# One change to a loop of 64 recurrent attention segments: order of scores and V, the last K in two banks, batched Q/K groups in 32-column tiles, and other issue times for three transfers

## The chip, the cores and the metric

The kernel runs on one core of a Trainium2 chip. The metric is device time of one execution in microseconds; before the change it is 854.24 us, the median of 3 runs (854.01 to 854.5).

The core has TensorE (matmul; its result goes to the eight banks of PSUM, each 512 fp32 values for each of 128 partitions), VectorE, ScalarE and GpSimd, which work on tiles in SBUF, and DMA queues. All transfers of this kernel are issued in program order by SyncE (SP). In the profile PE is TensorE's matmuls, PEld its weight loads, DVE is VectorE, ACT ScalarE, POOL GpSimd.

## What is computed

Two residual blocks in a row, A (attention with a small memory that is carried from segment to segment) and B (a gated MLP that mixes over the sequence). S = 2048 rows of 512, 32 heads of 128, 8 memory rows, segments of 32 rows: 64 segments that must run one after the other. Cut to what matters:

```python
def A(x, mem0, Wq, Wk, Wv, Wo):              # x: layernormed input
    mem = mem0
    for s in range(64):
        h = concat([mem, x[32 * s:32 * s + 32]])       # 8 + 32 rows
        q, k, v = h @ Wq, h @ Wk, h @ Wv               # 32 heads of 128
        p = softmax(mask(q @ k.T * 128 ** -0.5))       # memory columns open, the rest causal
        o = (p @ v) @ Wo
        mem = o[:8]
        out.append(o[8:])

def B(x, w_in, w_sp, b_sp, w_out):           # x: layernormed
    z = gelu(x @ w_in)                       # 512 -> 1792
    z2 = layernorm(z[:, 896:])
    return (z[:, :896] * (w_sp @ z2 + b_sp[:, None])) @ w_out

h = x + A(layernorm(x), ...)
out = h + B(layernorm(h), ...)
```

## The kernel before

All engines' programs are written out by hand, fully unrolled. A small emitter derives the semaphore waits: each operation names the tokens that it reads and writes (`reads=`, `writes=`, `after=`), and waits for their last writer or readers. Two engines that read one PSUM bank are also put in order. So each engine runs its operations in the order in which the Python code emits them.

**Layout.** A segment has 40 rows, 8 of memory and 32 of x. The loop works on 32 of them as one tile: the 8 memory rows and the first 24 rows of x (`hT`, transposed, 4 chunks `dc` of 128 of the 512 inputs). The last 8 rows of x of each segment ("extra rows") don't need the memory, so their Q, K and V are computed ahead for 16 segments at once, 128 rows: a "chunk" `ck`, 4 in all. Q and K of extra rows end in `QTx` (two buffers), V in DRAM (`vext_d`), from where `load_vx` brings one segment's rows into one of 3 slots of `Vx`.

**32-column tiles.** With 32 rows a weight tile has 32 columns, so four matmuls with `tile_position` (0, 32c) share the array, each with its own 512 columns: a "quad". `tile_mm` with `held` leaves out the weight load where the same `hT` chunk is loaded already.

**One turn of the loop** (L945 to L1112), in TensorE's order:

- `QK(s, b, mi, ...)`: Q (mi 0) and K (mi 1) of the heads' halves b = 0, 1, each four quads into its bank of `QKB`; between them the second half of `mem_out` brings the memory rows of the segment before. `QK_evac` copies a bank into `Tst` on ScalarE, with pairs of heads side by side as 4-byte words, and VectorE transposes 32x32 blocks of these words into `QT` and `KT`. The last K half (b = 1) is copied and transposed in two parts.
- `S_half(s, b)`: scores of a half, onto a mask that VectorE has put into the bank; `sm_exp` (ScalarE), `sm_sums` (matmuls with ones), `sm_ln` and `sm_rcp` (ScalarE; the reciprocal is exp(-ln)), `sm_norm` (GpSimd for half 0, VectorE for half 1; each a wide and a narrow multiplication).
- `V_half`: V of half b, four quads into banks 6 and 2; `V_evac` copies them on VectorE.
- one group of side work, from a list `gx`: in s = 1 to 7, 14 and 15 V of extra rows (`vx_group`), in the other turns below 48 Q or K of extra rows (`qkx_group`: 16 matmuls with 128-column weights of one head each and 128 moving rows), from 48 on a half row block of B's z2 (`z2_group`). Single quads of such work (`gv`) are poured in at one or two other places of a turn.
- `PV_half` for both halves, `cT_evac`, then `WoX_mm` (the output projection of extra rows, two quads), `Wo` into banks `OB` and `OB2`, `part_evac`, `mem_out`, and one more piece of side work by s mod 4.

**Transfers in the loop**, in SP's order: every second turn `wT_piece` transposes 64 rows of `B_w_sp` by DMA into `wst` and stores them to `wT_d` (32 pieces); rows of x and h; at the end of a turn V rows for s + 2; from s = 32 on B's weights and transposed rows. After the loop come `load_wT(0)` (the first quarter of the mixing weights, 8 transfers into what was w_q) and the z2 rows that had been stored.

Of the kernel before, what the change touches and what calls it, by code (L numbers as in the profile page):

```python
# [169 lines left out]
def fast_path(nc, st, keep, A_x, A_mem0, A_Wq, A_Wk, A_Wv, A_Wo, A_seg_len, B_w_in, B_w_sp, B_b_sp, B_w_out, out):  # L170
# [15 lines left out]
    CK = 16  # L186
# [24 lines left out]
    QTx = [region(4 * WSZ + i * QX, QX).rearrange("p (m s h k) -> p m s h k", m=2, s=CK, h=H) for i in range(2)]  # L211
# [206 lines left out]
    def qkx_evac(ck, i, bank, eng="act"):  # L418
        mi, h0 = i // 8, 4 * (i % 8)
        dst = QTx[ck % 2][:, mi, :, h0:h0 + 4, :].rearrange("p s h k -> p h s k")  # L420
# [60 lines left out]
    QKB = {(0, 0): 0, (0, 1): 1, (1, 0): 6, (1, 1): 7}  # L481
    SBK = (0, 1)
# [29 lines left out]
    def QK_evac(s, b, mi, parts=1):  # L512
        bank = QKB[(b, mi)]
        tb = mi
        n = 8 // parts
        for k in range(parts):
            tok = [("T", tb, 0), ("T", tb, 1)] if parts == 1 else [("T", tb, k)]
            cs = slice(64 * n * k, 64 * n * (k + 1))
            act(lambda e, cs=cs: e.activation(out=Tst[:, tb, cs].rearrange("p (hp i r) -> p hp i r", i=32, r=2),  # L519
                                              in_=ps[:, bank, cs].rearrange("p (hp r i) -> p hp i r", r=2, i=32), func=ACT.Copy),  # L520
                reads=[PB(bank)], writes=tok)
        for k in range(parts):
            tok = [("T", tb, 0), ("T", tb, 1)] if parts == 1 else [("T", tb, k)]
            src = Tst[:, tb, 64 * n * k:64 * n * (k + 1)].bitcast(U32)
            hs = slice(n * k, n * (k + 1))
            if mi == 0:
                dst = QT[:, b, hs, :, :].rearrange("p hp q r -> p (hp q r)").bitcast(U32).rearrange("p (hp q) -> p hp q", hp=n)[:, :, 8:40]
                wr = [("QT", b)]
            else:
                dst = KT[:, b, hs, :, :].rearrange("p hp q r -> p (hp q r)").bitcast(U32)  # L530
                wr = [("KT", b, 0), ("KT", b, 1)] if parts == 1 else [("KT", b, k)]
            dve(lambda e, dst=dst, src=src: e.transpose(out=dst, in_=src), reads=tok, writes=wr)  # L532
# [66 lines left out]

    def V_half(s, b, dcs=range(DC), held=None):  # L600
        bank = VB[b]
        sl = slot(s)
        for dc in dcs:
            for c in range(4):
                c0 = (16 * b + 4 * c) * DH
# [305 lines left out]
    for ck, i0 in ((1, 10), (2, 0), (3, 0)):  # L911
# [3 lines left out]
        for i in range(i0, 16):  # L915
            qkx_group(ck, i)
# [1191 lines left out]
```

## Time and profile before

| what | value |
|---|---|
| median of 3 runs | 854.24 us |
| the profiled execution, its own time | 853.86 us |
| its span in the profile | 851.7 us |
| busy: TensorE matmul | 837.0 us, 98% of the span |
| busy: VectorE | 538.8 us, 63% |
| busy: ScalarE | 427.1 us, 50% |
| busy: GpSimd | 159.8 us, 19% |
| mean DMA rate | 91 GB/s |
| loop: first scores of s = 1 to first scores of s = 63 | 57.67 to 686.76 us |
| granted TensorE clock | full in all slices |

The page's share of TensorE counts each matmul from its start to a modelled end, and matmuls of different tiles overlap. In the timeline a row is a run of like instructions with start, length and count; the distance from the start of one row to the start of the next is what the row cost.

### The profile page before, as it was taken

To read this page: it belongs to the slowest core of one execution; us is meant where nothing else is said; L and a number is where in the kernel's file an instruction comes from. 1 tells how busy PE (TensorE), PEld (TensorE's weight loads), DVE (VectorE), ACT (ScalarE), POOL (GpSimd) and SP (SyncE) were. 2 spreads that over 40 slices of the span, in tenths; PEclk is the share of its full clock that TensorE was granted. 3 is DMA by queue.
4 is the path that set the end of the run, shared out by engine and by line. 5 is a ranking of instruction groups with operands and counts; after the bars stand their busy time and mean duration, and the time that the engine had idled before them with its cause. 6 is when DMAs were issued, how large, how long until landed. Compare 5 with 4: busy or idle time off the path is not lost.

```text
span 851.7 us, 43893 instructions
## 1 busy us (share of the span) xinstructions
PE 837.0 (98%) x20921; PEld 447.0 (52%) x19133; DVE 538.8 (63%) x1256; ACT 427.1 (50%) x1151; POOL 159.8 (19%) x404
## 2 busy tenths in 40 slices
PE   6999999999999999999999999999999999999997
PEld 5754445555555555556555555555554544444443
DVE  3456677676666666676766666767666676553443
ACT  2455565656555655555655555565656566500000
POOL 5111121122121112121212121211112123200000
PEclk9999999999999999999999999999999999999999
DMA  9972322223212122121323222233322369032001
GB/s 319 379 227 59 75 56 57 54 47 82 57 34 75 34 65 62 26 72 47 64 58 85 55 74 51 81 70 85 91 57 80 96 184 366 2 112 105 33 12 40
DMA packets 105614, 77.21 MB, mean 91 GB/s; under 512 B 63304, under 2 KB 90960, under 8 KB 105424
## 3 DMA queue, kind: packets, MB, share of 16 engines
q1 hardware_dynamic: 105424, 74.35, 30.3%
q8 instruction: 159, 2.61, 1.3%
q14 instruction: 31, 0.25, 0.1%
HBM read 42.38 MB, written 21.59 MB: 75 GB/s over the span
## 4 chain that ended last, share of the span: by engine, by line
PE 95%; DMA 2%; SPq 1%; issue 0%; ACT 0%; DVE 0%; POOL 0%; POOLq 0%
PE f_ps L495 46%; PE f_ps L1183 11%; PE f_ps L496 8%; PE f_ps L414 6%; PE f_ps L707 4%; PE f_ps L1300 3%; PE f_ps L623 3%; PE f_ps L1176 2%; PE f_ps L433 2%; PE f_ps L775 2%; PE f_ps L554 1%; PE f_ps L575 1%; DMA f_arena<-in_A_Wk_dram 1%; PE f_ps L629 1%; PE f_ps L439 1%; PE f_ps L680 1%
## 5 line engine op out<-in xcount | busy, mean ns | idle before, releaser
L495 PE MATMUL f_ps<-f_arena,f_hT 128*32 128x512 bf16 x5120 | 359.5, 380 | 0.3
L495 PEld LDWEIGHTS f_ps<-f_arena,f_hT 128*32 128x32 bf16 x5120 | 117.0, 95 | 153.7 <-issue 63.0
L519 ACT ACTIVATE f_Tst<-f_ps 128x512 bf16<-128x512 f32 (+1 forms) x320 | 150.0, 510 | 77.5 <-PE f_ps L495 77.4
L495 PE MATMUL f_ps<-f_arena,f_cT 128*32 128x256 bf16 x3844 | 127.9, 272 | 0.7 <-ACT f_cT L642 0.5
L495 PEld LDWEIGHTS f_ps<-f_arena,f_cT 128*32 128x32 bf16 x3844 | 94.8, 96 | 27.3 <-ACT f_cT L642 18.2
L615 DVE CAST f_V_sb<-f_ps 128x512 bf16<-128x512 f32 x128 | 88.6, 692 | 25.4 <-PE f_ps L495 25.4
L1183 PE MATMUL f_ps<-f_arena 128*128 128x512 bf16 x448 | 100.9, 379 | 0.6 <-DMA f_arena<-wT_d 0.6
L532 DVE STREAM_TRANSPOSE f_QT<-f_Tst 128x256 uint32<-128x256 uint32 x128 | 57.0, 446 | 68.6 <-ACT f_Tst L519 68.5
L496 PE MATMUL f_ps<-f_arena,f_hT 128*32 128x512 bf16 x1024 | 99.8, 379 | 0.0
L539 POOL COPY f_QT<-f_arena 128x256 bf16<-128x256 bf16 x64 | 30.8, 482 | 313.3 <-PE f_ps L560 313.2
L642 ACT ACTIVATE f_cT<-f_ps 128x320 bf16<-128x320 f32 x128 | 49.0, 435 | 49.1 <-PE f_ps L629 49.1
L644 DVE TENSOR_SCALAR f_cT<-f_ps 128x320 bf16<-128x320 f32 x128 | 56.9, 487 | 25.4 <-PE f_ps L629 25.4
L532 DVE STREAM_TRANSPOSE f_KT<-f_Tst 128x128 uint32<-128x128 uint32 (+1 forms) x192 | 64.5, 349 | 12.9 <-ACT f_Tst L519 12.9
L1183 PEld LDWEIGHTS f_ps<-f_arena 128*128 128x128 bf16 x448 | 43.7, 98 | 53.4 <-DVE f_mv L723 1.0
L673 DVE CAST f_part<-f_ps 128x256 bf16<-128x256 f32 x64 | 27.2, 425 | 67.9 <-PE f_ps L495 67.9
L414 PE MATMUL f_ps<-f_hTe,f_arena 128*128 128x128 bf16 x1024 | 66.9, 223 | 2.2 <-DMA f_arena<-in_A_Wq_dram 1.4
L414 PEld LDWEIGHTS f_ps<-f_hTe,f_arena 128*128 128x128 bf16 x1024 | 59.1, 100 | 7.5 <-ACT f_hTe L395 1.6
L586 ACT ACTIVATE f_R_sb<-f_ps 128x160 f32<-128x160 f32 x128 | 39.1, 305 | 35.9 <-PE f_ps L496 32.7
L1189 DVE TENSOR_TENSOR f_arena<-f_ps,f_arena 128x512 f32<-128x512 f32 x28 | 19.3, 690 | 52.9 <-PE f_ps L1183 52.9
L685 ACT ACTIVATE f_hT<-f_ps 128x16 bf16<-128x16 f32 x126 | 23.3, 185 | 53.4 <-PE f_ps L680 53.0
L671 ACT ACTIVATE f_part<-f_ps 128x256 bf16<-128x256 f32 x64 | 24.6, 385 | 48.4 <-PE f_ps L495 48.4
L544 DVE CAST f_ps<-f_mask 128x224 f32<-128x224 bf16 x128 | 47.1, 368 | 0.0
(118 smaller groups left out, 1094.1 us busy)
## 6 DMA issues: line engine op xcount, KB each, us to landing
wT_d<-f_wst SPq DMA_DIRECT2D x32, 256.0 KB, 2.5
f_arena<-wT_d SPq DMA_DIRECT2D x32, 256.0 KB, 4.8
f_arena<-in_A_Wq_dram SPq DMA_DIRECT2D x4, 1024.0 KB, 8.7
f_arena<-in_A_Wk_dram SPq DMA_DIRECT2D x4, 1024.0 KB, 14.3
f_arena<-in_A_Wv_dram SPq DMA_DIRECT2D x4, 1024.0 KB, 14.5
f_arena<-in_A_Wo_dram SPq DMA_DIRECT2D x8, 512.0 KB, 9.5
f_Vx<-vext_d SPq DMA_DIRECT2D x63, 64.0 KB, 2.9
vext_d<-f_Vs SPq DMA_DIRECT2D x24, 128.0 KB, 2.0
```

The source lines that it names most:

```text
L414: pe(lambda e, h=h, dc=dc, hh=hh: e.matmul(ps[:, bank, hh * 128:(hh + 1) * 128], lhsT=ws[:, dc, h * DH:(h + 1) * DH], rhs=hTe[:, ck % 3, d ...
L495: return e.matmul(out, lhsT=lhsT, rhs=rhs, start=start, stop=stop, skip_group_check=True, tile_position=(0, 32 * c))
L496: return e.add_instruction(mybir.InstMatmult(name=nc.get_next_instruction_name(), ins=[e.lower_ap(rhs), e.lower_ap(lhsT)], outs=[e.lower_a ...
L519: act(lambda e, cs=cs: e.activation(out=Tst[:, tb, cs].rearrange("p (hp i r) -> p hp i r", i=32, r=2), in_=ps[:, bank, cs].rearrange("p (h ...
L532: dve(lambda e, dst=dst, src=src: e.transpose(out=dst, in_=src), reads=tok, writes=wr)
L544: dve(lambda e: e.tensor_copy(out=ps[:, bank, 0:224], in_=mask[:, :]), reads=["mask"], writes=[PB(bank)])
L586: act(lambda e: e.activation(out=R_sb[:, b, :], in_=ps[:, bank, 224:384], func=ACT.Ln, scale=LNS), reads=[PB(bank)], writes=[("R", b)])
L615: dve(lambda e: e.tensor_copy(out=V_sb[:, b, :], in_=ps[:, bank, :]), reads=[PB(bank)], writes=[("V", b)])
L642: act(lambda e: e.activation(out=dst, in_=src, func=ACT.Copy, scale=UNSC), reads=[PB(PVB[c])], writes=[("cT", c)])
L644: dve(lambda e: e.tensor_scalar(out=dst, in0=src, scalar1=UNSC, scalar2=None, op0=ALU.mult), reads=[PB(PVB[c])], writes=[("cT", c)])
L707: pe(lambda e, h=h, g=g, i=8 * qr + bg: e.matmul(ps[32 * g:32 * g + 32, WXB, :], lhsT=cTx[:, rb % 2, i, :], rhs=w_o[:, h, :], start=(i < 4 ...
L1183: pe(lambda e: e.matmul(ps[:, bank, 0:TB], lhsT=z2[:, sc, fb * 128:(fb + 1) * 128], rhs=wTb[tb % 2][:, :, sc, :], start=(n == 0), stop=(n ...
```

## The change

Seven edits, with the loop's mathematics unchanged:

1. **Order of the first QK quads.** Q and K of half 0 take chunk 0, then chunk 1, together, so that weights are held.
2. **K of half 1 in two banks** (`K1`, `K1_copy`, `K1_transpose`): 8 half-quads of 256 columns into banks 3 and 7 in place of four quads into bank 7.
3. **Order of scores, V and softmax.** Before the first sums stand four V quads (two chunks of half 0 less one, and one of half 1) in place of five, the last V quad of half 0 follows the second scores, the last one of half 1 the second sums. The second exp precedes the first ln.
4. **V copies and norms.** The copy of half 1 is split between VectorE and ScalarE; the narrow norm of half 0 goes from GpSimd to VectorE.
5. **Batched Q/K groups** (`qkr_group`): 36 of the 38 groups of extra rows in the loop take 32 rows of 4 segments and 16 heads as four quads of 512 columns, evacuated like QK by `pair_copy` on ScalarE and a transposition on VectorE. For this the heads are paired in another order, `QTx` has pairs side by side, and `qx_copy` moves 4-byte words.
6. **w_sp in halves.** 64 half pieces of 1024 columns, one a turn (two in s = 6 and 10), each issued after the first part of `Wo` of the turn before, each stored one turn later. V rows are issued at the start of the turn before their use.
7. **Mixing weights.** The first four transfers of `load_wT(0)` are issued in the last turn after the last Q, the others between the stored z2 rows.

```diff
-    QTx = [region(4 * WSZ + i * QX, QX).rearrange("p (m s h k) -> p m s h k", m=2, s=CK, h=H) for i in range(2)]
+    QTx = [region(4 * WSZ + i * QX, QX).rearrange("p (m s C g k r) -> p m s C g k r", m=2, s=CK, C=H // 8, g=4, r=2) for i in range(2)]
+    QTxU = [region(4 * WSZ + i * QX, QX).bitcast(U32).rearrange("p (m s hp k) -> p m s hp k", m=2, s=CK, hp=H // 2) for i in range(2)]
...
+    KB = (3, 7)
...
+    def K1(s, k, dc, first, last, held):
+        bank = KB[k] if s or k else 2
+        sl = slot(s)
+        for c in range(4):
+            rhs = w_k[:, dc, :].rearrange("p (h c i) -> p c h i", c=4, i=32)[:, c, 16 + 8 * k:24 + 8 * k, :]
+            pe(lambda e, c=c, rhs=rhs: tile_mm(e, ps[32 * c:32 * c + 32, bank, 0:256], hT[:, sl, dc, :], rhs, first, last, c, held),
+               reads=[("hTx", (s // 4) % 3), ("hTm", s, dc // 2), ("W", 1, 2), ("W", 1, 3)], writes=[PB(bank)])
+
+    def K1_copy(s, k):
+        bank = KB[k] if s or k else 2
+        act(lambda e: e.activation(out=Tst[:, 1, 256 * k:256 * k + 256].rearrange("p (gi r) -> p gi r", r=2),
+                                   in_=ps[:, bank, 0:256].rearrange("p (r gi) -> p gi r", r=2), func=ACT.Copy),
+            reads=[PB(bank)], writes=[("T", 1, k)])
+
+    def pair_copy(bank, tb):
+        act(lambda e: e.activation(out=Tst[:, tb, :].rearrange("p (C gi r) -> p C gi r", C=2, r=2),
+                                   in_=ps[:, bank, :].rearrange("p (C r gi) -> p C gi r", C=2, r=2), func=ACT.Copy),
+            reads=[PB(bank)], writes=[("T", tb, 0), ("T", tb, 1)])
...
-        src = QTx[buf][:, 0, j, :, :].rearrange("p (hp r) q -> p hp r q", r=2)
+        dst = QT[:].rearrange("p b hp q r -> p (b hp q r)").bitcast(U32).rearrange("p (hp q) -> p hp q", q=40)[:, :, 0:8]
+        src = QTxU[buf][:, 0, j, :, :]
...
-    def wT_piece(i):
-        sp(lambda e: e.dma_start_transpose(out=wst[:, :, :], in_=B_w_sp[i * 64:(i + 1) * 64, :]), writes=["wst"])
-        sp(lambda e: e.dma_start(wT_d[i], wst[:, :, :]), reads=["wst"], writes=[("wTd", i)])
+    def wT_in(p, after):
+        i, k = p // 2, p % 2
+        sp(lambda e: e.dma_start_transpose(out=wst[:, 8 * k:8 * k + 8, :], in_=B_w_sp[i * 64:(i + 1) * 64, 1024 * k:1024 * k + 1024]),
+           writes=[("wst", k)], after=after)
...
+    def qkr_group(ck, mi, b, r):
+        ws = (w_q, w_k)[mi]
+        def f():
+            for dc in range(DC):
+                for c in range(4):
+                    rhs = ws[:, dc, :].rearrange("p (h c i) -> p c h i", c=4, i=32)[:, c, 16 * b:16 * b + 16, :]
+                    pe(lambda e, dc=dc, c=c, rhs=rhs: tile_mm(e, ps[32 * c:32 * c + 32, XB, :], hTe[:, ck % 3, dc, 32 * r:32 * r + 32], rhs,
+                                                              dc == 0, dc == DC - 1, c),
+                       reads=[("hTe", ck % 3), ("W", mi, 2 * b), ("W", mi, 2 * b + 1)], writes=[PB(XB)])
+            def ev():
+                pair_copy(XB, 0)
+                dst = QTxU[ck % 2][:, mi, 4 * r:4 * r + 4, 8 * b:8 * b + 8, :].rearrange("p s hp k -> p hp s k")
+                dve(lambda e: e.transpose(out=dst, in_=Tst[:, 0, :].bitcast(U32)), reads=[("T", 0, 0), ("T", 0, 1)],
+                    writes=[("QTx", ck % 2, mi, 4 * b + r)])
+            return ev
...
+        if s > 0:
+            wT_step(s)
+        if 0 < s < NSEG - 1:
+            load_vx(s + 1)
...
+        QK(s, 1, 0, (2, 0, 1, 3), 2, 3, 2)
+        lastop["q"] = em.by_eng["pe"][-1]
+        QK_evac(s, 1, 0)
+        K1(s, 0, 3, True, False, True)
+        K1(s, 1, 3, True, False, True)
+        K1(s, 0, 0, False, False, False)
+        K1(s, 1, 0, False, False, True)
+        K1(s, 0, 1, False, False, False)
+        K1(s, 0, 2, False, True, False)
+        K1_copy(s, 0)
+        K1(s, 1, 2, False, False, True)
+        K1(s, 1, 1, False, True, False)
+        lastop["k"] = em.by_eng["pe"][-1]
+        K1_copy(s, 1)
...
-        V_half(s, 0, (1, 2, 3))
-        V_evac(0, "dve")
-        sm_sums(0)
-        sm_ln(0)
-        S_half(s, 1)
+            V_half(s, 0, (1, 2))
+            sm_sums(0)
+            S_half(s, 1)
+            V_half(s, 0, (3,))
+            V_evac(0)
...
         sm_exp(1)
+        sm_ln(0)
         sm_rcp(0)
...
+            V_half(s, 1, (3, 1), 3)
+            sm_sums(1)
+            V_half(s, 1, (2,))
...
         sm_norm(0, pool)
-        V_evac(1, "dve")
+        sm_normx(0)
+        V_evac(1, (0,))
+        V_evac(1, (1,), "act")
         sm_norm(1, dve)
+        sm_normx(1)
...
-        if s + 2 < NSEG:
-            load_vx(s + 2)
```

More of the change, by code (lines that the diff above doesn't have):

```diff
@@ L510, in QK @@
                    reads=[("hTx", (s // 4) % 3), ("hTm", s, dc // 2), ("W", mi, 2 * b), ("W", mi, 2 * b + 1)], writes=[PB(bank)])
[L512 to L532, printed above, removed]
@@ L602, in V_half @@
         sl = slot(s)
+        last = 2 if b and s else DC - 1
         for dc in dcs:
@@ L914, in fast_path @@
             vx_group(2, 1)
-        for i in range(i0, 16):
-            qkx_group(ck, i)
+        if i0:
+            qkx_group(ck, 10)
+            qkx_group(ck, 11)
+        for mi, b in ((0, 0), (0, 1), (1, 0), (1, 1))[3 if i0 else 0:]:
+            for r in range(4):
+                qkr_group(ck, mi, b, r)
     for ck, n0 in ((2, 2), (3, 0)):
@@ L929, in fast_path, with load_wT @@
     w_out = region(3 * WSZ + RB * 512, FB * D).rearrange("p (fb d) -> p fb d", fb=FB)
-    def load_wT(tb, after):
-        for t in range(8):
-            sp(lambda e, t=t: e.dma_start(wTb[tb % 2][:, t, :, :], wT_d[8 * tb + t]), reads=[("wTd", 8 * tb + t)],
+    def load_wT(tb, after, ts=range(8)):
+        for t in ts:
+            sp(lambda e, t=t: e.dma_start(wTb[tb % 2][:, t, :, :], wT_d[8 * tb + t]), reads=[("wTd", 8 * tb + t, 0), ("wTd", 8 * tb + t, 1)],
                writes=[("wT", tb % 2, t)], after=after)
```

94 lines of the change are left out of this document (65 added, 29 removed).

## The prediction

> **What bounds the kernel now.** I read the page first, then one loop turn (segment) in order of time: TensorE alone, then the three other engines, then the same place in a turn of each other kind.
>
> ```profile
> span 851.7 us, 43893 instructions
> ...
> PE 95%; DMA 2%; SPq 1%; issue 0%; ACT 0%; DVE 0%; POOL 0%; POOLq 0%
> ```
>
> The chain of waits that ended last is 95% TensorE, so only matmul work, or a short wait between matmuls, can change the time. The chain hides such waits because the trace's matmuls overlap: a wait shows as a longer distance from start to start. One turn of TensorE, s=25:
>
> ```profile
> 300.44 0.27 PE L554 MATMUL f_ps<-f_QT,f_KT 128*32 128x40 bf16 x16
> ...
> 301.65 0.24 PE L575 MATMUL f_ps<-f_E_sb,f_ones 128*32 128x160 bf16 x4
> 301.72 0.20 PE L496 MATMUL f_ps<-f_E_sb,f_ones 128*32 128x64 bf16 x4
> 301.75 0.27 PE L554 MATMUL f_ps<-f_QT,f_KT 128*32 128x40 bf16 x16
> ...
> 301.88 0.83 PE L495 MATMUL f_ps<-f_arena,f_hT 128*32 128x512 bf16 x12
> 302.56 0.25 PE L575 MATMUL f_ps<-f_E_sb,f_ones 128*32 128x160 bf16 x4
> 302.64 0.20 PE L496 MATMUL f_ps<-f_E_sb,f_ones 128*32 128x64 bf16 x4
> 302.78 1.07 PE L414 MATMUL f_ps<-f_hTe,f_arena 128*128 128x128 bf16 x16
> 303.78 0.27 PE L623 MATMUL f_ps<-f_E_sb,f_V_sb 32*128 32x40 bf16 x16
> ...
> 303.99 0.28 PE L623 MATMUL f_ps<-f_E_sb,f_V_sb 32*128 32x40 bf16 x16
> ...
> 304.26 0.61 PE L707 MATMUL f_ps<-f_arena,f_cTx 128*32 128x512 bf16 x8
> ...
> 304.92 1.05 PE L495 MATMUL f_ps<-f_arena,f_cT 128*32 128x256 bf16 x32
> 305.79 0.28 PE L496 MATMUL f_ps<-f_arena,f_cT 128*32 128x256 bf16 x4
> ...
> 310.55 0.27 PE L554 MATMUL f_ps<-f_QT,f_KT 128*32 128x40 bf16 x16
> ```
>
> The turn is 310.55 - 300.44 = 10.11 us. I count from its first score block, "S0" (300.44). A score block takes 301.88 - 301.75 = 0.13. From S0's end (300.57) to the sums at 301.65 stand five V quads (four column tiles of 512 columns): 1.08 / 5 = 0.216 each. Now the losses. (a) Three V quads from 301.88 should take 0.65 and take 0.68: the second sums wait for the second exp. (b) The last sums matmuls take 0.03 before another block with 32-column tiles (301.72 to 301.75) and 0.14 before the 128-column group L414: 0.11 for the change of tile form. (c) L414 takes 1.00. (d) The first PV block takes 0.21, the second 0.27. What the last two wait for is in the other engines:
>
> ```profile
> 300.66 0.66 ACT L519 ACTIVATE f_Tst<-f_ps 128x256 bf16<-128x256 f32 x2 [0.27 <-PE f_ps L495]
> 301.21 0.36 ACT L568 ACTIVATE f_E_sb<-f_ps 128x224 bf16<-128x224 f32 x1
> 301.96 0.31 ACT L586 ACTIVATE f_R_sb<-f_ps 128x160 f32<-128x160 f32 x1 [0.39 <-PE f_ps L496]
> 302.16 0.35 ACT L568 ACTIVATE f_E_sb<-f_ps 128x224 bf16<-128x224 f32 x1
> 302.41 0.33 ACT L590 ACTIVATE f_R_sb<-f_R_sb 128x160 f32<-128x160 f32 x1
> 302.88 0.30 ACT L586 ACTIVATE f_R_sb<-f_ps 128x160 f32<-128x160 f32 x1
> 303.22 0.34 ACT L590 ACTIVATE f_R_sb<-f_R_sb 128x160 f32<-128x160 f32 x1
> ```
> ```profile
> 301.08 0.59 DVE L532 STREAM_TRANSPOSE f_KT<-f_Tst 128x128 uint32<-128x128 uint32 x2 [0.20 <-ACT f_Tst L519]
> ...
> 302.75 0.69 DVE L615 CAST f_V_sb<-f_ps 128x512 bf16<-128x512 f32 x1 [0.18 <-PE f_ps L495]
> 303.59 0.34 DVE L594 TENSOR_TENSOR f_E_sb<-f_R_sb,f_E_sb 128x160 bf16<-128x160 f32 x1
> 303.86 0.21 DVE L598 TENSOR_TENSOR f_E_sb<-f_R_sb,f_E_sb 128x64 bf16<-128x64 f32 x1
> ```
> ```profile
> 302.88 0.49 POOL L594 TENSOR_TENSOR f_E_sb<-f_R_sb,f_E_sb 128x160 bf16<-128x160 f32 x1 [0.21 <-ACT f_R_sb L590]
> ```
>
> Hand-over times follow. Matmuls to ScalarE 0.21 (sums end 301.75, L586 at 301.96); ScalarE to TensorE 0.05 (exp ends 302.51, sums 302.56); ScalarE to VectorE 0.03 (303.56 to 303.59); VectorE to TensorE 0.06 (303.93 to 303.99); ScalarE to GpSimd 0.14. So the second PV block starts when the second normalisation L594 ends: sums, ln, reciprocal and norm set it, and TensorE has nothing to fill the time.
>
> **The change, part by part.** *Order of scores and V.* One V quad fewer stands before the first sums and second scores, and one comes after the second sums. Times after S0, first with every hand-over in time: S0 ends 0.13; four quads, sums at 0.99 (before: 1.21); second scores 1.09 to 1.22; three V quads, second sums at 1.87 (before: 2.12) to 1.97; the last V quad to 2.19.
>
> Is the smaller cover enough? The K copies and exp come first. K's last half is now two banks: 8 half-quads of 256 columns, and the first bank is complete two half-quads (0.22) before S0. Its copy runs 0.00 to 0.38 instead of from 0.22, the second starts 0.28 later (0.66 for the pair less 0.38) and ends at 0.66, its transposition runs to 1.00, and with 0.06 the second scores can start at 1.06; TensorE comes at 1.09. The exp follows from 0.55 to 0.91, its sums can start at 0.96, TensorE comes at 0.99. So both covers hold, with 0.03 to spare; every 0.01 beyond that costs 0.6 us over the 63 turns. Exp of the second scores goes ahead of the first ln: 1.43 to 1.78, sums possible at 1.83 < 1.87, so (a) goes, 0.03.
>
> The 256-column half-quads cost a little: the 32 matmuls at 304.92 take 0.87 where four whole quads take 0.86, so +0.01 a turn.
>
> *Batched groups.* A Q/K group of 16 matmuls of 128 columns becomes four quads, 0.86, and its tile form is that of its neighbours: the change (b) goes, and the one to PV's own form stays, taken as 0.10, like (b). L414's 1.00 + 0.11 become 0.96. The evacuation becomes a ScalarE copy and a VectorE transposition. It frees VectorE and lies in ScalarE's idle time behind the PV copies; with a second 512-wide copy there one turn in four, it ends just before the copy that the recurrence needs. Cost nothing; without that cover, what it exceeds by, in a quarter of 36 turns. The transposition's split write and the GpSimd copy in 4-byte words aren't in the trace; nearest are the QT transposition and today's copy, whose results nobody wants before the next turn: nothing. The first groups' copies, before the loop, now write every second element; nothing shows that either, and they are taken as they are.
>
> *V copies, norms.* With the group, TensorE reaches the first PV block at 2.19 + 0.86 + 0.10 = 3.15 (before: 3.34). ln of the first half starts 0.25 behind the exp (as 302.16 to 302.41), 1.68, reciprocal 2.02 to 2.35, GpSimd's norm 2.49 to 2.98: in time. Second half: ln 2.24 (ScalarE free), reciprocal 2.58 to 2.92, norm 2.95 to 3.29, PV at 3.35; TensorE is there at 3.30. The V halves:
>
> ```profile
> L673 DVE CAST f_part<-f_ps 128x256 bf16<-128x256 f32 x64 | 27.2, 425 | 67.9 <-PE f_ps L495 67.9
> ...
> L671 ACT ACTIVATE f_part<-f_ps 128x256 bf16<-128x256 f32 x64 | 24.6, 385 | 48.4 <-PE f_ps L495 48.4
> ```
>
> VectorE: small norm 2.38 to 2.59, V half 0.43 from about 2.53 to 2.95. The ScalarE half reads the same bank and so waits for it: 3.00 to 3.39, ready at 3.44, and the second half of PV's matmuls wants it at about 3.40. So a wait of 0.04 to 0.09 remains in that block, and the block after it (L707) starts at about 3.64 against 3.82: **0.18 a turn**. Bounds: with all waits gone 0.28; with the second PV wait 0.1 longer, 0.08.
>
> The other turns have their own filling between sums and PV:
>
> ```profile
> 588.98 0.27 PE L623 MATMUL f_ps<-f_E_sb,f_V_sb 32*128 32x40 bf16 x16
> ...
> 589.24 0.27 PE L623 MATMUL f_ps<-f_E_sb,f_V_sb 32*128 32x40 bf16 x16
> ```
> ```profile
> 81.26 0.27 PE L623 MATMUL f_ps<-f_E_sb,f_V_sb 32*128 32x40 bf16 x16
> ...
> 81.41 0.28 PE L623 MATMUL f_ps<-f_E_sb,f_V_sb 32*128 32x40 bf16 x16
> ```
>
> In a turn with a z2 group the first PV block takes 0.26, in one with a V group 0.15: the latter fills the wait already. z2 turns so gain 0.03 of (a), 0.11 of the first block, and some 0.03 of the second, whose last matmuls wait for the small norm (304.07 + 0.06 against 303.99 + 0.10): 0.17. V turns gain 0.04. The two Q/K groups that stay 128 wide gain 0.12.
>
> *DMA.* The pieces of w_sp, the V rows and the mixing weights move on SP's queue.
>
> ```profile
> f_Vx<-vext_d SPq DMA_DIRECT2D x63, 64.0 KB, 2.9
> ...
> f_wst<-in_B_w_sp_dram SPq DMA_TRANSPOSE x32, 4.3
> ```
> ```profile
> PE f_ps L1183 <- DMA f_arena<-wT_d: 0.6, 1, 0.6
> PE f_ps L433 <- issue: 0.3, 1, 0.3
> ```
>
> 64 half transpositions and 64 stores replace 32 and 32. Each waits at the head of SP's queue for the output projection of the turn before, which is over when the queue comes there; behind it stand V rows wanted over 10 us later (they take 2.9), the x rows and the h stores: nothing waits. Half of the mixing weights start at the last Q instead of behind the last V and four rows of z2, so L1183's 0.6 goes: 0.5. The wait for issue (instructions that hadn't come) stands once in the list; whether shorter transpositions disturb that fetch less or their number more I can't see: from -1 to +1, taken as 0.3 gained.
>
> *Sum.* 36 x 0.18 = 6.5; 16 x 0.17 = 2.7; 9 x 0.04 = 0.4; 2 x 0.12 = 0.2; less 63 x 0.01 = 0.6; end 0.5; fetch 0.3: 10.0. The profiled execution took 853.86 (span 851.7 and 2.2 around it), so 843.9 by it; the runs' median is 0.4 above that one, so **844.2**.
>
> **Rivals.** *The PV wait grows.* If the ScalarE half of V, last in a queue of exp, two ln and two reciprocals, is 0.1 later than worked out, 52 turns lose 5.2: 849.4. For it: two engines hand one bank over, which no row shows. Against: ScalarE stands idle there now, from 303.56 on.
>
> *All waits go.* Then 36 turns gain 0.10 more, and fetch 0.8: 839.8. Against: the norm's 3.35 is TensorE's 3.30 plus 0.05, at best.
>
> *It gives back what it gains.* The same V half 0.2 late: 0.18 less 0.2, and z2 turns too; about 854.
>
> *Slower: the pair copies.* All copies out of PSUM for Q and K now take their pair from 512 bytes apart, today from 128.
>
> ```profile
> L519 ACT ACTIVATE f_Tst<-f_ps 128x512 bf16<-128x512 f32 x192 | 107.8, 596 | 60.7 <-PE f_ps L495 60.7
> ...
> L451 ACT ACTIVATE f_Vs<-f_ps 128x512 bf16<-128x512 f32 x15 | 8.9, 595 | 1.4 <-PE f_ps L433 0.8 <-PE f_ps L439 0.6
> ```
>
> At 128 bytes a copy costs as much as one that reads in order (596 and 595 ns). If 512 bytes doubled the cost per element, a 256-wide copy would take 0.60 (0.38 + 0.22, the 0.22 being 0.60 - 0.38), the second would end at 1.09, its transposition at 1.43, and the second scores come at 1.49, 0.40 late: 63 x (0.40 - 0.18) = 13.9 lost, some 867. It decides from 0.1 us more per copy, since two copies stand in line and 0.03 is spare. The Trainium skill, "PSUM — Partial Sum Buffer", Specifications, says that PSUM has 8-byte lines and that an access that isn't contiguous slows matmuls much; by it such copies should lose already, and the two rows, 1 ns apart, don't show that for ScalarE. I keep 0.08 for it.
>
> **How the numbers follow.** Forecast 0.62 (844.2, its own range 841 to 847); PV wait grows 0.16 (849.4); all waits go 0.07 (839.8); gives back 0.06 (854); slower copies 0.09 (867). A measurement here tells 0.2% (1.7 us) from no change. Faster: 0.62 + 0.16 + 0.07 = 0.85; same 0.05; slower 0.10, with a little of the fourth case. The range 839.5 to 851 leaves out the last two cases and part of the tails.
>
> **What would show it.** From S0 to the second sums 1.87 us (2.12 now); L707 3.64 after S0 (3.82); no 0.11 behind the second sums; turns of 9.9 us with Q/K and z2 groups and 10.05 with V groups. Wrong: second scores or first sums that start later than 0.13 + 0.86 and 0.10 after S0, pair copies over 0.65, a PV block behind ScalarE's V copy by more than 0.1, or more waits of TensorE for issue.

## The result, and the profile after

| what | before | after |
|---|---|---|
| median of 4 runs each, one series | 854.18 us (854.01 to 854.5) | 844.5 us (843.97 to 844.92) |
| the profiled execution, its own time | 853.86 us | 844.12 us |
| its span | 851.7 us | 842.4 us |

The ratio is 0.988, with a 95% interval from 0.9868 to 0.9891: 9.7 us faster, where 844.2 was forecast. The head of the page after the change: first the span, then busy time, share and instructions of each engine, then the chain that ended last by engine.

```profile
span 842.4 us, 44608 instructions
...
PE 827.5 (98%) x21945; PEld 424.5 (50%) x18629; DVE 524.2 (62%) x1320; ACT 469.1 (56%) x1251; POOL 127.4 (15%) x340
...
PE 96%; DMA 1%; SPq 1%; issue 0%; DVE 0%; ACT 0%
```

TensorE still carries the chain (96%). ScalarE took over from VectorE the copies of the batched groups (36 of some 0.6 us) and half of the second V copy (64 of some 0.4 us); it went from 50% to 56% and has 0% of that chain. The turn to compare with s=25 of before, TensorE's timeline (start, length, engine, line, operation, tile sizes, count):

```profile
289.12 0.27 PE L568 MATMUL f_ps<-f_QT,f_KT 128*32 128x40 bf16 x16
...
290.11 0.24 PE L589 MATMUL f_ps<-f_E_sb,f_ones 128*32 128x160 bf16 x4
...
290.21 0.27 PE L568 MATMUL f_ps<-f_QT,f_KT 128*32 128x40 bf16 x16
...
291.00 0.25 PE L589 MATMUL f_ps<-f_E_sb,f_ones 128*32 128x160 bf16 x4
291.08 0.20 PE L498 MATMUL f_ps<-f_E_sb,f_ones 128*32 128x64 bf16 x4
291.11 0.39 PE L497 MATMUL f_ps<-f_arena,f_hT 128*32 128x512 bf16 x4
291.32 1.04 PE L497 MATMUL f_ps<-f_arena,f_hTe 128*32 128x512 bf16 x16
292.29 0.27 PE L642 MATMUL f_ps<-f_E_sb,f_V_sb 32*128 32x40 bf16 x16
292.42 0.21 PE L648 MATMUL f_ps<-f_E_sb,f_Vx 32*128 32x64 bf16 x4
292.49 0.31 PE L642 MATMUL f_ps<-f_E_sb,f_V_sb 32*128 32x40 bf16 x16
292.64 0.20 PE L648 MATMUL f_ps<-f_E_sb,f_Vx 32*128 32x64 bf16 x4
292.76 0.62 PE L726 MATMUL f_ps<-f_arena,f_cTx 128*32 128x512 bf16 x8
...
299.06 0.27 PE L568 MATMUL f_ps<-f_QT,f_KT 128*32 128x40 bf16 x16
```

The turn is 299.06 - 289.12 = 9.94 us (10.11 before). From its S0 at 289.12: first sums 0.99, second scores 1.09, second sums 1.88, extra-rows projection (L707 before, now L726) 3.64. The change of tile form behind the second sums is gone: their last row starts at 291.08 and the next quad 0.03 later (0.14 before). The group of 16 matmuls takes 292.29 - 291.32 = 0.97 with the change of form behind it. The two PV blocks stand 0.20 apart (292.29, 292.49); before it was 0.21. The same stretch on ScalarE and on VectorE:

```profile
289.12 0.66 ACT L524 ACTIVATE f_Tst<-f_ps 128x256 bf16<-128x256 f32 x2
...
291.73 0.34 ACT L604 ACTIVATE f_R_sb<-f_R_sb 128x160 f32<-128x160 f32 x1
292.14 0.38 ACT L632 ACTIVATE f_V_sb<-f_ps 128x256 bf16<-128x256 f32 x1
```
```profile
291.68 0.42 DVE L634 CAST f_V_sb<-f_ps 128x256 bf16<-128x256 f32 x1
292.11 0.33 DVE L608 TENSOR_TENSOR f_E_sb<-f_R_sb,f_E_sb 128x160 bf16<-128x160 f32 x1
292.35 0.22 DVE L614 TENSOR_TENSOR f_E_sb<-f_R_sb,f_E_sb 128x64 bf16<-128x64 f32 x1
```

ScalarE's V half ends at 292.52 and VectorE's narrow norm at 292.57, so the second L642 block spends 0.15 instead of 0.13, and the narrow products behind it start at 292.64, 0.07 after the norm. The block itself starts at 292.49, 0.05 behind the end of VectorE's wide norm (292.44) and 0.20 behind the first block, where V turns, which fill this wait, needed 0.15 before the change. These two waits are what is left ahead of the projection in this turn, and ScalarE and VectorE end within 0.05 of each other. The groups by line (columns as in the page: count, busy us, mean ns of one, idle before and its releaser) answer the question of the pair copies:

```profile
L534 ACT ACTIVATE f_Tst<-f_ps 128x512 bf16<-128x512 f32 x228 | 129.4, 597 | 60.5 <-PE f_ps L497 60.5
...
L524 ACT ACTIVATE f_Tst<-f_ps 128x256 bf16<-128x256 f32 x128 | 42.1, 381 | 3.7
...
L553 POOL COPY f_QT<-f_arena 128x128 uint32<-128x128 uint32 x64 | 18.7, 292 | 298.5 <-PE f_ps L574 298.4
```

597 ns with the pair 512 bytes apart against 596 with it 128 bytes apart: no difference. GpSimd's copy in 4-byte words fell from 482 to 292 ns. TensorE's waits (us in total, times, longest):

```profile
PE f_ps L497 <- issue: 0.6, 1, 0.6
...
PE f_ps L380 <- issue: 0.5, 1, 0.5
PE f_ps L648 <- issue: 0.5, 2, 0.3
```

The wait for wT_d is gone, and waits for issue have grown from 0.3 and 0.2 to 0.6, 0.5 and 0.5. From the starts of all score blocks, the lengths of the turns (medians of a kind), and what single turns exceed their median by, added up:

```
                                   before   after
Q/K groups in 32-column tiles      10.119    9.947   (s = 16 to 39; 40 to 47: 10.093 and 9.924)
Q/K groups 128 wide                10.118   10.01
z2 groups                          10.096    9.935
V groups                           10.082   10.060
sum over the medians, s = 1 to 62    2.6      3.6 us
S0 of s = 1 at                      57.67    57.29 us
from S0 of s = 63 to the end       164.95   163.95 us
```

### The profile page after: what moved, and what is told of

Read it like the earlier page. It is cut to its first block, busy times and chain, and to the rows that moved or that the text cites. A ratio compares the mean times of both kernels' runs of the same rounds, so it can differ in the third digit from the quotient of the medians.

```text
span 842.4 us, 44608 instructions
## 1 busy us (share of the span) xinstructions
PE 827.5 (98%) x21945; PEld 424.5 (50%) x18629; DVE 524.2 (62%) x1320; ACT 469.1 (56%) x1251; POOL 127.4 (15%) x340
## 3 DMA queue, kind: packets, MB, share of 16 engines
q8 instruction: 161, 2.64, 1.4%
## 4 chain that ended last, share of the span: by engine, by line
PE 96%; DMA 1%; SPq 1%; issue 0%; DVE 0%; ACT 0%
PE f_ps L497 44%; PE f_ps L498 14%; PE f_ps L1272 11%; PE f_ps L726 4%; PE f_ps L1389 3%; PE f_ps L1265 3%; PE f_ps L642 3%; PE f_ps L434 2%; PE f_ps L794 2%; PE f_ps L415 2%; PE f_ps L568 1%; DMA f_arena<-in_A_Wk_dram 1%; PE f_ps L589 1%; PE f_ps L440 1%; PE f_ps L699 1%; PE f_ps L648 1%
## 5 line engine op out<-in xcount | busy, mean ns | idle before, releaser
L497 PE MATMUL f_ps<-f_arena,f_hT 128*32 128x512 bf16 (+1 forms) x4616 | 353.5, 356 | 0.8 <-issue 0.6
L498 PE MATMUL f_ps<-f_arena,f_hT 128*32 128x512 bf16 x2552 | 206.7, 336 | 0.0
L534 ACT ACTIVATE f_Tst<-f_ps 128x512 bf16<-128x512 f32 x228 | 129.4, 597 | 60.5 <-PE f_ps L497 60.5
L634 DVE CAST f_V_sb<-f_ps 128x512 bf16<-128x512 f32 (+1 forms) x128 | 71.1, 555 | 42.1 <-PE f_ps L497 42.1
L582 ACT ACTIVATE f_E_sb<-f_ps 128x224 bf16<-128x224 f32 x128 | 46.2, 361 | 36.5 <-PE f_ps L574 36.5
L553 POOL COPY f_QT<-f_arena 128x128 uint32<-128x128 uint32 x64 | 18.7, 292 | 298.5 <-PE f_ps L574 298.4
L604 ACT ACTIVATE f_R_sb<-f_R_sb 128x160 f32<-128x160 f32 x128 | 43.1, 337 | 4.0
L524 ACT ACTIVATE f_Tst<-f_ps 128x256 bf16<-128x256 f32 x128 | 42.1, 381 | 3.7
L683 POOL COPY f_cTx<-f_cT 128x256 bf16<-128x256 bf16 x64 | 25.4, 396 | 121.8 <-DVE f_cT L663 121.8
```

The lines of the kernel that those rows point to most:

```text
L497: return e.matmul(out, lhsT=lhsT, rhs=rhs, start=start, stop=stop, skip_group_check=True, tile_position=(0, 32 * c))
L498: return e.add_instruction(mybir.InstMatmult(name=nc.get_next_instruction_name(), ins=[e.lower_ap(rhs), e.lower_ap(lhsT)], outs=[e.lower_a ...
L524: act(lambda e: e.activation(out=Tst[:, 1, 256 * k:256 * k + 256].rearrange("p (gi r) -> p gi r", r=2), in_=ps[:, bank, 0:256].rearrange(" ...
L534: act(lambda e: e.activation(out=Tst[:, tb, :].rearrange("p (C gi r) -> p C gi r", C=2, r=2), in_=ps[:, bank, :].rearrange("p (C r gi) -> ...
L582: act(lambda e: e.activation(out=E_sb[:, b, :], in_=ps[:, bank, 0:224], func=ACT.Exp, scale=scale, bias=SHIFT), reads=[PB(bank)], writes=[ ...
L604: act(lambda e: e.activation(out=R_sb[:, b, :], in_=R_sb[:, b, :], func=ACT.Exp, scale=-1.0, bias=RBIAS), reads=[("R", b)], writes=[("R", b)])
```

## The experiments

All but one, which is the changed kernel once more, are edits of the changed kernel, timed against the kernel before in four series (its medians there: 854.33 to 854.77 us). The new order of the first QK quads (edit 1) has no run of its own.

### Groups of extra rows 128 wide again

```diff
-        if i0:
-            qkx_group(ck, 10)
-            qkx_group(ck, 11)
-        for mi, b in ((0, 0), (0, 1), (1, 0), (1, 1))[3 if i0 else 0:]:
-            for r in range(4):
-                qkr_group(ck, mi, b, r)
+        for i in range(i0, 16):
+            qkx_group(ck, i)
```

> The changed kernel with all 36 batched groups back in the 128-column form; all else as changed. Theory of the prediction: the order of scores and V brings most of a turn's 0.17 us, and the group's form 0.06 (0.15 shorter, of which the PV wait gives 0.09 back). So Q/K turns of 10.01 in place of 9.95, 36 x 0.06 = 2.2 more: 846.7 us. Rival: the form is the gain (0.11 for the change of tile form and 0.04 of work, 36 x 0.15 = 5.4): 850.

Measured: 846.84 us (845.65 to 848.02), ratio 0.9907 (0.9893 to 0.9922). The Q/K turns take 10.013 us, the z2 turns stay at 9.93. So the tile form of the groups is worth 10.013 - 9.947 = 0.066 us a turn, 2.4 us in 36 turns; the other 0.106 of the 0.172 stays with the other edits, as the theory had it.

### The old order of scores, V and softmax

```diff
-            V_half(s, 0, (1, 2))
+            V_half(s, 0, (1, 2, 3))
+            V_evac(0)
             sm_sums(0)
+            sm_ln(0)
             S_half(s, 1)
-            V_half(s, 0, (3,))
-            V_evac(0)
...
         sm_exp(1)
-        sm_ln(0)
+        if s == 0:
+            sm_ln(0)
...
-            V_half(s, 1, (3, 1), 3)
+            V_half(s, 1, (3, 1, 2), 3)
             sm_sums(1)
-            V_half(s, 1, (2,))
```

> The changed kernel with scores, V and softmax in the old order (five V quads before the first sums, the first ln before the second exp, no V quad after the second sums); groups, V copies, K banks and transfers as changed. Theory: the chain of the second sums, ln, reciprocal and norm sets PV, and with the old order a shorter group only waits longer: second sums 2.1 after the first scores, L-line of the extra rows' projection 3.8 after them as before the change, 52 turns lose 0.17: 853 us. Rival: the shorter group brings its 0.15 by itself: 847.

Measured: 850.95 us (850.73 to 852.03), ratio 0.996 (0.9946 to 0.9974): between the two. The turns settle it: 10.107, 10.08 and 10.088 us for Q/K, z2 and V, as in the kernel before. TensorE at s=25:

```profile
291.12 0.27 PE L568 MATMUL f_ps<-f_QT,f_KT 128*32 128x40 bf16 x16
...
294.32 0.28 PE L642 MATMUL f_ps<-f_E_sb,f_V_sb 32*128 32x40 bf16 x16
...
294.65 0.27 PE L642 MATMUL f_ps<-f_E_sb,f_V_sb 32*128 32x40 bf16 x16
...
294.92 0.61 PE L726 MATMUL f_ps<-f_arena,f_cTx 128*32 128x512 bf16 x8
```

With the new groups and copies TensorE comes to the first PV block at 3.20 after S0 (3.34 before the change), but the second stands 0.33 behind it and L726 comes at 3.80: what the group gave was lost in the next wait. Taking the new order out costs 0.16 us a turn, and the group's 0.07 shows only with it. The total is lower than the turns say. The profiled execution, the slowest of five, is 1.8 us below that of the kernel before: 0.6 from the turns, 0.4 at the end, 0.2 ahead of the loop, 0.3 outside the span and 0.3 from fewer late instructions. The median lies another 1.1 us lower, which the one profile doesn't explain.

### The last K in one bank

```diff
-        K1(s, 0, 3, True, False, True)
-        K1(s, 1, 3, True, False, True)
...
-        K1(s, 1, 1, False, True, False)
-        K1_copy(s, 1)
+        QK(s, 1, 1, (3, 0, 1, 2), 3, 2, 3)
+        for k in range(2):
+            K1_copy_one(k)
```

> The changed kernel with the last K half in one bank as four whole quads, copied in two parts after all of it. Theory: the copies start 0.22 later, the second scores come at 1.28 after the first in place of 1.09, and the turn gets 0.18 longer: 63 x 0.18 = 11 more, 856 us. Rival: the cover of four V quads is long enough without it, and the 0.01 of the half-quads is saved: 843.9.

Measured: 856.82 us (855.19 to 858.6), ratio 1.0024 (1.0014 to 1.0033): with this one edit taken out the changed kernel is slower than the kernel before. Turns: 10.139, 10.124 and 10.253 us (Q/K, z2, V), +0.19 each. TensorE and ScalarE:

```profile
293.77 0.27 PE L574 MATMUL f_ps<-f_QT,f_KT 128*32 128x40 bf16 x16
...
294.33 0.60 PE L497 MATMUL f_ps<-f_arena,f_hT 128*32 128x512 bf16 x8
294.95 0.25 PE L595 MATMUL f_ps<-f_E_sb,f_ones 128*32 128x160 bf16 x4
```
```profile
294.00 0.66 ACT L530 ACTIVATE f_Tst<-f_ps 128x256 bf16<-128x256 f32 x2 [0.27 <-PE f_ps L497]
294.54 0.36 ACT L588 ACTIVATE f_E_sb<-f_ps 128x224 bf16<-128x224 f32 x1
```

Two quads from 294.33 should be over at 294.76; the first sums start at 294.95. The exp stands behind both K copies on ScalarE, and these start only 0.23 after the scores (294.00 against 293.77); the exp ends at 294.90, 0.05 ahead of the sums. The second bank is what lets one quad less stand ahead of the sums.

### The V copies: both old forms, then each alone

```diff
-        sm_normx(0)
-        V_evac(1, (0,))
-        V_evac(1, (1,), "act")
+        sm_normx(0, pool)
+        V_evac(1)
```

> The changed kernel with V's half 1 copied whole on VectorE and the narrow norm of half 0 on GpSimd again. Theory: VectorE's copy runs to 3.11 after the first scores and the wide norm ends at 3.39 in place of 3.29, so PV's second block comes 0.1 later, less the 0.04 that it now waits for ScalarE's half: 52 x 0.06 to 0.1, 3 to 5 more: 848 to 850 us. Rival: the split only moves work: 844.5.

Measured: 854.91 us (854.02 to 856.89), ratio 1.0011 (1.0001 to 1.002), turns of 10.146, 10.124 and 10.125 us: 0.20 and 0.19 a turn with Q/K and z2 groups, 0.06 with V groups. That is at least twice what was expected. So the two edits were taken apart. V's half copied whole, narrow norm on VectorE:

> Half of the earlier experiment with both old forms: V's second half copied whole on VectorE, the narrow multiplication of block 0 stays on VectorE. Theory (VectorE's own chain between the V copies and the second values product sets its end): the chain gets longer by 0.692 - 0.419 = 0.27 us a turn, of which 0.07 was slack (it ends at 292.567 and the product that needs it started at 292.64), so 0.20 us a turn and 844.5 + 63 x 0.20 = 857 us. Rival (each old form carries half of the 0.20 us that both together cost): 0.10 us a turn, 851 us.

Measured: 851.27 us (850.64 to 851.63), ratio 0.9963 (0.995 to 0.9975); turns 10.114 us, +0.167. The kind of cost is the theory's, its size lies between the two. VectorE and TensorE:

```profile
303.30 0.68 DVE L634 CAST f_V_sb<-f_ps 128x512 bf16<-128x512 f32 x1
303.90 0.32 DVE L608 TENSOR_TENSOR f_E_sb<-f_R_sb,f_E_sb 128x160 bf16<-128x160 f32 x1
304.13 0.22 DVE L614 TENSOR_TENSOR f_E_sb<-f_R_sb,f_E_sb 128x64 bf16<-128x64 f32 x1
```
```profile
300.73 0.27 PE L568 MATMUL f_ps<-f_QT,f_KT 128*32 128x40 bf16 x16
...
304.27 0.27 PE L642 MATMUL f_ps<-f_E_sb,f_V_sb 32*128 32x40 bf16 x16
304.41 0.21 PE L648 MATMUL f_ps<-f_E_sb,f_Vx 32*128 32x64 bf16 x4
```

The second PV block starts 0.05 behind the wide norm (304.22), its narrow products 0.06 behind the narrow one (304.35): VectorE sets both. The norm starts 0.08 before the recorded end of the copy; in the changed kernel it starts at its end, because it waits for the reciprocal (over at 292.07 there, norm at 292.11). So the narrow norm ends 3.62 after S0 (300.73) in place of 3.45: the chain grew by 0.17 and not by 0.27, 0.1 that the expectation had not counted. Of the 0.07 that it had counted as slack, 0.06 is the hand-over, which stays. The other half, the narrow norm of block 0 on GpSimd:

> The other half: the narrow multiplication of block 0 on GpSimd behind the wide one, V's second half in two halves as in the changed kernel. Theory: GpSimd is through with the wide one at 292.14 and the narrow one takes 0.30 to 0.35 us there, so the first narrow values products start at about 292.50 and not at 292.42; VectorE is 0.22 us earlier and waits for nothing; 0.08 us a turn, 849.5 us. Rival (each carries half): 0.10 us a turn, 851 us. If VectorE's chain is what held the second product all along, and GpSimd's narrow one costs under 0.2 us: no change or a gain, 843 to 844.5 us.

Measured: 852.06 us (851.02 to 853.57), ratio 0.9969 (0.9958 to 0.9981); turns 10.100 us, +0.153, twice the theory's. GpSimd, VectorE and TensorE:

```profile
305.03 0.37 POOL L614 TENSOR_TENSOR f_E_sb<-f_R_sb,f_E_sb 128x64 bf16<-128x64 f32 x1
```
```profile
304.91 0.33 DVE L608 TENSOR_TENSOR f_E_sb<-f_R_sb,f_E_sb 128x160 bf16<-128x160 f32 x1
305.16 0.33 DVE L614 TENSOR_TENSOR f_E_sb<-f_R_sb,f_E_sb 128x64 bf16<-128x64 f32 x1
```
```profile
305.11 0.27 PE L642 MATMUL f_ps<-f_E_sb,f_V_sb 32*128 32x40 bf16 x16
305.46 0.21 PE L648 MATMUL f_ps<-f_E_sb,f_Vx 32*128 32x64 bf16 x4
```

The first narrow products start at 305.46, 0.35 behind the block's start (0.13 in the changed kernel), 0.06 after GpSimd's end at 305.40. Where the two engines' multiplications lie over one another, both are longer: VectorE's narrow one 0.33 and not 0.22, GpSimd's 0.37 and not 0.31 (308 ns in the kernel before). So each edit alone costs 0.15 to 0.17 and both together 0.20: they aren't two costs that add but two paths to the same PV blocks, of which the later counts.

### w_sp pieces whole and V rows at the end of a turn

```diff
-        if s > 0:
-            wT_step(s)
-        if 0 < s < NSEG - 1:
-            load_vx(s + 1)
...
+        if s % 2 == 1 and s < NSEG - 1:
+            wT_piece(s // 2)
+        if s == NSEG - 2:
+            wT_piece(NWT - 1)
...
+        if s + 2 < NSEG:
+            load_vx(s + 2)
```

> The changed kernel with whole pieces of w_sp every second turn and V rows issued two turns ahead, as before the change. Theory: these transfers lie beside TensorE and touch only how often it waits for instructions; turns without such a wait stay at 9.95 (Q/K) and 9.93 (z2), the sum of the long turns' excess goes from 3.6 to between 2 and 4: 843 to 845 us. Rival: the new times shorten the turn itself, then turns over 9.97 and 846 or more.

Measured: 845.43 us (844.49 to 847.29), ratio 0.9887 (0.9872 to 0.9901). Median turns as in the changed kernel, sum over the medians 5.1 us. The time lies between the theory's 843 to 845 and the rival's 846, the sum above the theory's 2 to 4; 0.9 us from the changed kernel is too little to tell: inconclusive on the transfers, clear in that they don't set the median turn.

### The transposing transfers replaced by plain ones

```diff
-        sp(lambda e: e.dma_start_transpose(out=wst[:, 8 * k:8 * k + 8, :], in_=B_w_sp[i * 64:(i + 1) * 64, 1024 * k:1024 * k + 1024]),
+        sp(lambda e: e.dma_start(wst[:, 8 * k:8 * k + 8, :], B_w_sp[i // 2 * 128:i // 2 * 128 + 128, 512 * (2 * (i % 2) + k):512 * (2 * (i % 2) + k) + 512].rearrange("p (a b) -> p a b", b=64)),
```

> Leaves out the transposition of w_sp: the same 64 loads of 128 KB at the same places, as plain copies of 128 rows by 512 columns, so the mixing weights hold other numbers. Theory (the transposing transfers hold up the instruction fetch): the sum of the turns over their medians falls from 3.6 to under 2 us, 842.5 to 843.2 us, median turns unchanged at 9.95 and 9.93 us. Rival (the fetch stalls whatever else is moved): sum 3 to 4 us, 844.5 us.

Measured: 844.6 us (844.19 to 845.18), ratio 0.9885 (0.9869 to 0.9902), sum over the medians 3.9 us. The theory falls: the long turns come without any transposition of w_sp too.

### The changed kernel once more

> The changed kernel once more, nothing edited, so that its long turns can be compared in a second profile. Theory (TensorE waits for its instructions at fixed places of the program): 844.5 us, and turns over their median by 0.3 us or more stand at the same turns as in the first profile (the largest at turn 11), with a sum over the medians of 3 to 4 us. Rival (they fall at random): other turns, and a sum anywhere between 2.4 and 5.1 us, the ends seen so far.

Measured: 844.1 us (843.67 to 845.59), ratio 0.9879 (0.9863 to 0.9896), sum over the medians 4.2 us. The largest excess stands in the turn from s=10 to 11 again: 1.0 us in the first profile, 0.86 here, 0.6 with plain transfers, and 0.9 in the kernel with V groups behind the projection (below). It is there in every profile of the changed kernel and its edits, between 0.55 and 1.23 us, and not in the kernel before, whose turn 10 is at its median. TensorE there, in the changed kernel's first profile and in its second:

```profile
154.33 0.39 PE L497 MATMUL f_ps<-f_arena,f_hT 128*32 128x512 bf16 x2
155.34 0.39 PE L497 MATMUL f_ps<-f_arena,f_hT 128*32 128x512 bf16 x2 [0.61 <-issue]
```
```profile
154.47 0.39 PE L497 MATMUL f_ps<-f_arena,f_hT 128*32 128x512 bf16 x2
155.36 0.39 PE L497 MATMUL f_ps<-f_arena,f_hT 128*32 128x512 bf16 x2 [0.49 <-issue]
```

TensorE stops between two matmuls of one quad, which wait for the same data. Other long turns agree only in part: s=22 is long in both (by 0.69 and 0.38) and so is s=60 (by 0.4), s=16 and s=44 only in the second. So the place in the program counts, as the theory has it, and whether a place stalls, and for how long, also differs from run to run, as the rival has it.

### The mixing weights loaded behind the loop again, twice

```diff
-            load_wT(0, [lastop["q"]], range(4))
             xn2T_dma(8, [xops[s]])
-            for r in range(2):
-                z2_back(r, r + 1, lastop["v"])
-            load_wT(0, [], range(4, 8))
-            for r in range(2, 4):
+            for r in range(4):
                 z2_back(r, r + 1, lastop["v"])
...
+    load_wT(0, [lastop["q"]])
     for r in range(4, NP):
```

> The changed kernel with the first mixing weights issued behind the loop again. Theory: TensorE waits 0.5 to 0.6 us for them at the first mixing matmul: 845.0 to 845.2 us. Rival: the end is shorter for another reason and the wait stays away: 844.5.

> The kernel with the mixing weights' loads behind the loop again, unedited, a second time. Theory (with the loads behind the loop the first mixing products hang on transfers that land late by an amount that differs from run to run): median again 845 to 847.5 us and the single runs spread over 3 us or more. Rival (the spread of 5.3 us the first time was that stretch of time alone): 844.6 to 845.2 us with a spread of 1 to 1.5 us, like the changed kernel's.

Measured: 847.0 us (844.72 to 849.98), ratio 0.9911 (0.9891 to 0.9932), and the second time 845.85 us (844.89 to 847.08), ratio 0.9894 (0.9879 to 0.9909). Both medians lie above the changed kernel's 844.1 to 844.5; the spread was 5.3 and 2.2 us, against 1.0 and 1.9 in the changed kernel's two series, so whether the scatter belongs to the kernel stays open. The cost itself stands in the profiles: from S0 of s = 63 to the end the two profiles take 165.70 and 165.83 us, the changed kernel's two 163.95 and 163.79. SP's queue and TensorE in the second of them:

```profile
687.17 3.77 SPq L993 DMA_DIRECT2D f_arena<-wT_d  x8
```
```profile
697.79 1.24 PE L1269 MATMUL f_ps<-f_arena 128*128 128x512 bf16 x5 [2.13 <-DVE f_xo L750]
```

And in the changed kernel:

```profile
677.80 1.75 SPq L993 DMA_DIRECT2D f_arena<-wT_d  x4
...
682.80 1.88 SPq L993 DMA_DIRECT2D f_arena<-wT_d  x4
```
```profile
694.43 1.24 PE L1272 MATMUL f_ps<-f_arena 128*128 128x512 bf16 x5
```

The first mixing product waits 2.13 us (1.43 in the first of the two kernels; the kernel before 0.56). The view names VectorE's `f_xo`, in the first kernel `f_mv`; the product reads neither, only normalised rows of z2 and the mixing weights. So the transfers have to be read one by one. In the second kernel the sixth, issued at 689.56, lands at 694.64, and the seventh, issued at 690.03, takes, by the view of the tile wT_d in that stretch:

```profile
DMA to landing us min/median/max: 7.0/7.0/7.0
```

It lands at 697.04; the eighth has no landing recorded, and the product starts at 697.79. In the first kernel the seventh lands at 696.26, the eighth again has no landing, and the product starts at 697.70. In the kernel before the eighth lands at 703.52 and the product starts at 703.62. In the changed kernel the last one lands at 689.92, 4.5 us ahead of the product. The DMA packets fill the gap: the 1024 of 2048 bytes that these eight transfers consist of have ended by 697.23 and 696.57 in the two kernels, 0.56 and 1.13 us ahead of the product, by 703.18 in the kernel before (0.44 ahead) and by 689.49 in the changed one. So the old place leaves the product hanging on the last of these transfers, clearly in the second kernel and less so in the first, and the new place gives it 4.5 us to spare. What held the seventh transfer up wasn't separated.

### V groups: the spare quads behind the projection

```diff
             return lambda: vx_evac(ck, n, XB, "dve")
-        f.full = False
+        f.full = True
```

> A try at a version that beats both: in the turns with a V group (4 to 7, 14 and 15) the spare V matmuls stand behind the extra-rows projection, as they already do in the Q/K turns, and no longer ahead of the values products. Theory: there TensorE waits 0.16 us for the first copy of the products before the output projection, which these 4 matmuls of 0.22 us would cover; these six turns fall from 10.06 to about 9.95 us, 0.66 us in all, 843.4 to 843.9 us beside 844.1 and 844.5 us. Rival: the copy out of the V bank then comes late for the next user of its bank, turns stay at 10.06 us and the time at 844.1 to 844.5 us.

Measured: 843.8 us (842.89 to 845.49), ratio 0.9879 (0.9861 to 0.9896). The turns do what the theory says: s = 4 to 7, 14 and 15 fall from 10.06 to 9.945 us, 0.7 us in all. In the total that can't be told from the changed kernel, whose own runs lie 1.9 us apart. It is at least no slower, and it is the version that I would keep.

## Why the prediction was right, point by point

| term | forecast | in the profiles before and after |
|---|---|---|
| 36 batched Q/K turns, with the half-quads taken off | 6.1 | 6.2 (4 x 0.171 + 24 x 0.172 + 8 x 0.169) |
| 16 z2 turns | 2.6 | 2.6 (16 x 0.161) |
| 9 V turns | 0.3 | 0.2 (7 x 0.022 + 2 x 0.017) |
| 2 turns with 128-wide groups | 0.2 | 0.2 |
| end, without the last z2 turn | 0.5 | 0.8 (1.00 - 0.16) |
| instructions that come late | 0.3 | -1.0 (2.6 to 3.6) |
| ahead of the loop | 0 | 0.4 (57.67 to 57.29) |
| outside the span | 0 | 0.4 (2.16 to 1.72) |
| sum | 10.0 | 9.8, measured 9.74 |

- **The turn.** Every step came at the time worked out, within 0.02: first sums 0.99, second scores 1.09, second sums 1.88 (1.87), first PV block 3.17 (3.15), second 3.37 (3.35), projection 3.64. It rested on hand-over times read from one turn of before and on durations of like instructions. The 0.03 of cover that the prediction gave the K copies fits: with one bank they start 0.23 later against the scores, and the turn loses 0.19.
- **Which edit earns it.** The prediction booked 0.18 as one sum from order, groups and copies. Single edits undone cost 0.07 (groups), 0.16 (order), 0.19 (second K bank), 0.17 (split V copy) and 0.15 (narrow norm) a turn: together 0.74, four times the gain. They are links of one chain, and any of four missing gives all or nearly all of it back.
- **PV wait grows; gives back.** Both fell: ScalarE's V half ends 292.52, 3.40 after S0, where 3.39 was worked out. **All waits go** fell too, since 0.05 to 0.1 remains.
- **Slower pair copies.** The 256-wide copies take 381 ns, and the rival needed 0.60 us. The sentence on non-contiguous access in the Trainium skill, "PSUM — Partial Sum Buffer", Specifications, is about matmuls, and no run here shows it for ScalarE's reads. The prediction gives this rival a chance of 0.08 in one place and 0.09 in another; the forecast hangs on neither.
- **The end.** The wait for the mixing weights went, as predicted, but was under-sized at 0.5: with their old place in the changed kernel it is 1.4 and 2.1 us.
- **Fetch: the step that failed.** "Taken as 0.3 gained", inside bounds of -1 to +1, came out at the bound of loss, 1.0, and 1.6 in the second profile. The suspicion behind it, that transpositions disturb the fetch, fell too: without them the sum over the medians is 3.9 us. What the runs show in its place is late instruction blocks at fixed places (last section).
- **What was chance.** The missing 1.3 was mostly made good by terms that nobody had forecast. Ahead of the loop, the changed kernel's second profile has 57.67 us, the old value; outside the span the profiled runs of this study took from 1.7 to 2.3 us. The forecast's closeness of 0.3 us is partly luck; the turn terms, 9.2 of the 10, are not.

## What to carry to other kernels

Where a chain runs through four engines inside each turn, work out each hand-over from the start of the turn before editing, and test which links end within 0.1 us of one another: such edits don't add, they only pay together. Where a view names an operation for a wait that the waiting instruction doesn't read, look up the transfers that it does read. In a fully unrolled program the place of an instruction can decide a stall, so a median turn and the sum of what turns exceed it by are kept apart.

## What the runs showed of the hardware

**Instructions that come late.** In the changed kernel's two profiles the 62 turns exceed their medians by 3.6 and 4.2 us, much of it in waits for issue inside runs of like matmuls. Counting TensorE's records in order of their start (matmuls, weight loads and its sequencer's own), the large stall of turn 10 follows number 7617 in both profiles, with plain transfers and with the V groups moved, and others in one or more of these runs follow 11201, 14785, 21953, 25537, 27841, 29121 and 37313: all a whole number of 256 apart. The instruction queue's row of the DMA view of the changed kernel (packets, MB, share of 16 engines):

```profile
q8 instruction: 161, 2.64, 1.4%
```

161 packets and 2.64 MB are 16.4 KB each; TensorE's 40,744 records make 159 blocks of 256. The Trainium skill, "Runtime: NRT & Kernel Launch", Instruction fetch mechanics, says that instructions are streamed in blocks of 16 KiB, 256 instructions each, and that the cost of crossing a boundary is mostly hidden. The packet size and the spacing of 256 agree. Most crossings are hidden here too, but one cost 1.0 us in the changed kernel.

The times of the 16,384-byte packets tie the stalls to the fetch. The fourteen profiles have 1,997 such places in their loops. At 71 of them TensorE's next instruction starts over 0.24 us after the one before, with issue named as the reason, and it starts 1.22 to 1.60 us after the end of the last packet; over all places this distance is 2.4 us in the median and never under 1.19. The only other stops of that length for issue in the loops are the changes of tile form ahead of 128-column groups, 0.31 us each. So a place stalls when its packet comes late: ahead of these 71 stalls the packet starts 1.6 us after the place before, in the median, and 0.8 us where nothing stalls. No run took the fetch away, and why a packet starts late, most often in turn 10, stays open.

**VectorE and GpSimd side by side.** With both engines multiplying SBUF operands at one time, VectorE's narrow multiplication went from 222 to 328 ns (means of the run) and GpSimd's from 308 to 370. The Trainium skill, "SBUF — State Buffer", SBUF: two separate sides, says that such a VectorE operation with two SBUF inputs and a GpSimd operation hold a shared port in turn. The trace agrees in that both grow and that they end one behind the other: GpSimd's 0.16 after VectorE's wide one (305.24), VectorE's narrow one 0.09 after GpSimd's. That one waits out the whole of the other isn't shown, since these remainders are shorter than the 0.31 and 0.22 that each takes alone.
